# The first 512 tokens of x, loaded two tokens to a partition

## The chip, the cores and the metric

The kernel runs on one core of a Trainium2 chip. The metric is the device time of one launch in microseconds (us). The core has five engines with an instruction stream each: TensorE (PE; its weight loads are shown apart as PEld), VectorE (DVE), ScalarE (ACT), GpSimd (POOL) and SyncE (SP). SP and ACT also issue the DMA transfers, which 16 DMA engines carry out.

## The reference

The computation mixes a memory-augmented attention layer and a gated feed-forward layer, token by token, with a gate. There are 2048 tokens of width 512 in bf16; the attention has 32 heads of width 16 and 4 segments of 512 tokens, the feed-forward a width of 1792.

```python
x = A_x                                                # 2048 x 512
g = sigmoid((x * gate_w).sum(-1, keepdims=True))
a = attention(x)                                       # below
b = (gelu(x @ w_gate) * (x @ w_up)) @ w_down
out = g * a + (1 - g) * b
# attention: q, k, v = x @ wq, x @ wk, x @ wv, in 32 heads; for each segment s of 512 tokens:
p = softmax(q_s @ k_s.T / 4 + causal mask);  a_dot = p @ v_s
a_mem = phi(q_s) @ M / (phi(q_s) @ z + 1e-6)           # phi(t) = t + 1 if t > 0 else exp(t)
o_s = sigmoid(beta) * a_mem + (1 - sigmoid(beta)) * a_dot
M += phi(k_s).T @ v_s;  z += phi(k_s).sum(0)
a = concat(o_s) @ wo
```

## The kernel before

The work goes segment by segment (512 tokens each): projections to q, k and v, scores and softmax, memory, feed-forward, output. Every step is a task with the buffers that it reads and writes. The order in which tasks are given to the engines is written out by hand in a long string, `ORDER` (line 1004), with the PSUM bank or the engine behind a colon: `xev0_00:a` is the task `xev0_00` on ScalarE, `xev0_03:d` is one on VectorE. Each engine runs its own tasks in that order. From the buffers' keys the class `Emitter` works out the semaphore waits of each instruction; it waits for every key that it reads.

All weight matrices lie in SBUF with the contraction index on partitions. Each segment's x is needed transposed, as `xT[...]`: width on partitions (4 blocks `kb` of 128), tokens in the columns. Segments 1 to 3 get it by transposing DMA loads (`ld_xt`, line 355). The first segment is loaded as it is, and TensorE transposes it, which is the part that the change touches:

- Lines 361 and 362: four loads, `x0_0` to `x0_3`, of 128 tokens each (128 KB) into the staging buffer `pt[5]`, a tile of 128 partitions by 4 by 512. Load q puts token 128q + p on partition p, in the q-th 512 columns: 1024 bytes to a partition. The loads 0 and 2 are issued on SP, 1 and 3 on ACT. Each writes the key `("xs", q)`.
- Lines 363 to 367: `wk` in three loads (`wk0` on SP, `wk1` on ACT, 128 KB each; `wk2`, 256 KB, on SP), then `wq` in two loads on SP. By `ORDER`, SP issues x0_0, wk0, x0_2, wk2, wq0, wq1, then wv, which waits for x0_2, and ACT issues x0_1, wk1, x0_3.
- Lines 391 to 393: `wake`, nine matmuls of constants on TensorE ahead of everything else.
- `turn_x0` (line 895): for each half h of the segment (256 tokens) and each block kb, a task `xtr0_{h}{kb}` of two transposes on TensorE (q = 2h and 2h + 1) into two neighbouring 128-column pieces of PSUM, and a task `xev0_{h}{kb}` that copies the 256 columns to `xT[0][:, kb, 256h : 256h + 256]` (line 907 on ScalarE, line 908 on VectorE).
- `project` (line 499): for the first segment, the tasks `K0_k0` to `K0_k3` (line 504) multiply block i of `wk` with the first half's 256 columns, one task for each block i, into four banks; `K0_0b` to `K0_3b` (line 510) do the same for the second half. K0_k0 needs wk0, K0_k1 wk1, K0_k2 and K0_k3 need wk2.

On TensorE the order is wake, the eight transposes of the first half, K0_k0, K0_k1, the eight of the second half, K0_k2, K0_k3, then the K0_*b tasks, the projections to q (line 482) and so on. On ScalarE it is xev0_00, xev0_01, xev0_02, xev0_13, xev0_11; on VectorE xev0_03, xev0_10, xev0_12.

Of the kernel before, what the change touches and what calls it, by code (L numbers as in the profile page):

```python
# [252 lines left out]
def _build(es, nc, A_x, A_wq, A_wk, A_wv, A_wo, A_beta, B_w_gate, B_w_up, B_w_down, gate_w, out):  # L253
    def sb(name, shape, dtype=BF):
        return es.enter_context(nc.sbuf_tensor(name, shape, dtype))
# [4 lines left out]
    xT = [sb(f"xT{i}", [P, 4, 512]) for i in range(R_XT)]  # L260
# [12 lines left out]
    pt = [sb(f"pt{i}", [P, 4, 512]) for i in range(R_PT)]  # L273
# [10 lines left out]
    ident = sb("ident", [P, P])  # L284
# [33 lines left out]
    def program(exact):  # L318
# [3 lines left out]
        def task(name, ways, lat):  # L322
            return S.add(Task(name, ways, lat))

        def one(name, eng, est, instrs, lat=None):
            if lat is None:
                lat = {PE: L_PE, ACT: L_ACT, DVE: L_DVE, POOL: L_POOL, SP: 0.0}[eng]
            return S.add(Task(name, [(eng, est, instrs)], lat))
# [7 lines left out]
        def load(name, eng, fn, writes, issue=0.52, lat=2.5, size=0.0, wait=()):  # L336
            t = one("ld_" + name, eng, issue, [I(fn, [*wait, *late], [*writes, ("ld", name)], sem("s_" + name))],
                    lat=lat)
            t.size = size
# [7 lines left out]
        stage = (R_PT - 1,)  # L347
# [4 lines left out]
        def ld_w(name, eng, dst, src, writes, size, wait=()):  # L352
            load(name, eng, lambda e: e.dma_start(dst, src), writes, size=size, wait=[("ld", w) for w in wait])  # L353
# [5 lines left out]
                    x_of(s % R_XT, kb), issue=1.31, size=0.28, wait=[("ld", behind)])  # L359

        for q, eng in enumerate((SP, ACT, SP, ACT)):
            ld_w(f"x0_{q}", eng, pt[stage[0]][:, q, :], A_x[0, 128 * q:128 * q + 128, :], [("xs", q)], 0.125)
        for h, (eng, c) in enumerate(((SP, slice(0, 1)), (ACT, slice(1, 2)), (SP, slice(2, 4)))):
            ld_w(f"wk{h}", eng, wk[:, c, :], wsrc(A_wk)[:, c, :], [("wk", i) for i in range(c.start, c.stop)],
                 0.125 * (c.stop - c.start))
# [529 lines left out]
        def turn_x0():  # L895
            xs = pt[stage[0]]
            xbf = XALL.bitcast(BF)
            for h in range(2):
                for kb in range(4):
                    key, at = ("Xq", kb), 1024 * kb  # L900
                    one(f"xtr0_{h}{kb}", PE, 2 * T_TR, [I(lambda e, q=q, kb=kb, at=at + 128 * (q % 2): e.transpose(
                        xbf[:, at:at + 128], xs[:, q, kb * 128:(kb + 1) * 128], ident[:, :]),
                        [("xs", q), ("pt", stage[0]), ("ident",)], [key]) for q in (2 * h, 2 * h + 1)])
                    dst, src = xT[0][:, kb, 256 * h:256 * h + 256], xbf[:, at:at + 256]
                    wr = [("xT", 0, kb, 2 * h), ("xT", 0, kb, 2 * h + 1)]
                    task(f"xev0_{h}{kb}", [
                        (ACT, 0.33, [I(lambda e, dst=dst, src=src: e.activation(dst, src, ACTF.Copy), [key, ("X", s0)], wr)]),
                        (DVE, 0.2, [I(lambda e, dst=dst, src=src: e.tensor_copy(dst, src), [key, ("X", s0)], wr)])], L_DVE)

        turn_x0()  # L910
        head_gates()
        for s in range(NSEG):
# [15 lines left out]
        return S, outs  # L928

    S, outs = program(False)  # L930
    order = S.schedule()
    parts = []
    for turn_ in (order, program(True)[0].in_turn()):
        began = {e: len(em.streams[e]) for e in ENGINES}
        for t, eng, instrs in turn_:
            for spec in instrs:
                em.plan(eng, spec)
        parts.append({e: slice(began[e], len(em.streams[e])) for e in ENGINES})
# [175 lines left out]
```

## Time and profile before

| | us |
|---|---|
| Median of 3 runs (265.3, 265.38, 657.67) | 265.38 |
| The profiled execution | 265.2 |
| Its span, first to last instruction | 263.5 |
| TensorE busy in the span | 254.5 |
| ScalarE busy in the span | 209.6 |
| VectorE busy in the span | 204.3 |
| GpSimd busy in the span | 95.7 |

The profile shows one execution. Times in it count from the start of the span, 1.7 us less than the execution as a whole. A row of the timeline gives start, duration, engine, line (L901 is line 901 of the kernel), operation, output and input tiles, and, in brackets, how long the engine sat idle before it and what ended that. `SPq` and `ACTq` are the DMA issues of SP and ACT. The chain of waits follows the work that ended last back from the last instruction: at each step to what released it, or to the instruction before it on its engine. A row by line gives the shortest, median and longest duration in ns. The windows view gives, for a stretch of time, the busy time of each engine in the order PE, PEld, DVE, ACT, POOL, the granted clock of TensorE, the mean busy share of the DMA engines and the GB/s that they moved. Tile names leave out buffer numbers: `pt<-in_A_x_dram` is a load of x into the staging buffer.

### The profile page before, as it was taken

What the parts mean: (1) busy time and instruction counts of PE and PEld (TensorE: products, weight loads), DVE (VectorE), ACT (ScalarE), POOL (GpSimd) and SP (SyncE); (2) the same over time, 40 slices, a digit from 0 to 9 for tenths busy, and PEclk for the clock granted to TensorE, in tenths of its full rate; (3) what the DMA queues carried; (4) which work ended last, traced back from release to release, by engine and by line L of the source; (5) the groups of instructions that cost most, each with busy time, mean ns of one, the idle gap of its engine ahead of it and who ended that gap; (6) DMA issues with size and microseconds to landing.
All of it is one profiled execution on the core that took longest, in us unless ns stands there. A gap on an engine that the chain in (4) does not pass through costs nothing.

```text
span 263.5 us, 6622 instructions
## 1 busy us (share of the span) xinstructions
PE 254.5 (97%) x2792; PEld 113.3 (43%) x2830; DVE 204.3 (78%) x391; ACT 209.6 (80%) x174; POOL 95.7 (36%) x159
## 2 busy tenths in 40 slices
PE   8999999999999999999999999999999999999995
PEld 4633434444344453434434344444344443434343
DVE  1756672989969578998799987797889596877775
ACT  4488989989898998999989697749879988387512
POOL 6007405062643206017262737422734036153600
PEclk9999999999999999999999999999999999999999
DMA  7987179910047301001003000000001000000102
GB/s 225 251 171 215 38 109 203 252 51 2 0 73 106 51 15 40 2 24 40 2 11 74 0 2 2 26 27 2 0 29 49 2 0 2 22 20 2 40 2 85
DMA packets 24702, 14.95 MB, mean 57 GB/s; under 512 B 14558, under 2 KB 24158, under 8 KB 24670
## 3 DMA queue, kind: packets, MB, share of 16 engines
q1 hardware_dynamic: 24094, 14.04, 24.1%
q8 instruction: 23, 0.38, 0.6%
q10 hardware_dynamic: 576, 0.46, 0.5%
q14 instruction: 9, 0.07, 0.1%
HBM read 8.14 MB, written 2.10 MB: 39 GB/s over the span
## 4 chain that ended last, share of the span: by engine, by line
PE 90%; DVE 5%; issue 2%; DMA 2%; SPq 0%
PE psD L482 49%; PE psD L830 19%; PE psX L638 8%; PE psD L691 7%; PE psD L847 5%; DVE gb L817 2%; DMA wk<-in_A_wk_dram 2%; PE psD L510 1%; DVE ost L851 1%; DVE tT L552 1%; SPq L353 0%; DVE phk L495 0%; PE psD L579 0%; PE psD L451 0%; PE psX L597 0%
## 5 line engine op out<-in xcount | busy, mean ns | idle before, releaser
L654 ACT ACTIVATE pt<-psX 128x2048 bf16<-128x2048 f32 x72 | 135.2, 1877 | 30.2 <-PE psX L638 28.5
L660 POOL TENSOR_TENSOR pt<-pt,ctri 128x256 bf16<-128x256 bf16 x128 | 90.5, 714 | 152.8 <-ACT pt L654 148.2
L482 PE MATMUL psD<-xT,wu 128*128 128x512 bf16 x213 | 54.6, 380 | 1.5 <-issue 1.1
L482 PE MATMUL psD<-xT,wg 128*128 128x512 bf16 x216 | 53.5, 380 | 1.0 <-issue 0.6
L830 PE MATMUL psD<-wd,gb 128*128 128x512 bf16 x217 | 53.0, 379 | 0.9 <-issue 0.8
L817 DVE TENSOR_TENSOR gb<-psD,gb 128x512 bf16<-128x512 f32 x56 | 37.3, 683 | 9.4 <-PE psD L482 9.3
L552 DVE STREAM_TRANSPOSE tT<-psD 128x512 f32<-128x512 f32 x35 | 24.2, 707 | 14.7 <-PE psD L691 12.0
L830 PEld LDWEIGHTS psD<-wd,gb 128*128 128x128 bf16 x224 | 20.7, 98 | 26.0 <-issue 2.8
L482 PEld LDWEIGHTS psD<-xT,wg 128*128 128x128 bf16 x224 | 20.5, 98 | 26.3 <-issue 2.6
L482 PEld LDWEIGHTS psD<-xT,wu 128*128 128x128 bf16 x224 | 20.1, 98 | 25.8 <-issue 3.7
L638 PE MATMUL psX<-qT,kD 32*128 32x192 bf16 (+7 forms) x512 | 28.5, 287 | 0.0
L638 PEld LDWEIGHTS psX<-qT,kD 32*128 32x128 bf16 x512 | 8.2, 92 | 25.7 <-ACT pt L654 21.1
L691 PE MATMUL psD<-pt,vnat 64*17 64x128 bf16 (+7 forms) x512 | 18.8, 283 | 0.0
L703 DVE SCALAR_TENSOR_TENSOR ob<-tT,gq,rcall 128x256 bf16<-128x256 f32 x32 | 17.9, 559 | 1.1
L691 PE MATMUL psD<-pt,vsh 64*17 64x128 bf16 (+7 forms) x512 | 18.3, 283 | 0.0
L851 DVE SCALAR_TENSOR_TENSOR ost<-psD,gtok,wds 128x512 bf16<-128x512 f32 (+1 forms) x18 | 12.2, 685 | 6.4 <-PE psD L847 6.2
L482 PE MATMUL psD<-wv,xT 128*128 128x512 bf16 x63 | 16.7, 380 | 0.2 <-issue 0.2
L482 PE MATMUL psD<-xT,wq 128*128 128x512 bf16 x58 | 15.6, 379 | 0.8 <-issue 0.6
L847 PE MATMUL psD<-wo,oT 128*128 128x512 bf16 (+1 forms) x69 | 15.5, 355 | 0.5 <-issue 0.3
L691 PEld LDWEIGHTS psD<-pt,vnat 64*17 64x17 bf16 x512 | 11.6, 86 | 8.6 <-POOL pt L660 3.8
L808 ACT ACTIVATE gb<-psD 128x512 bf16<-128x512 f32 x28 | 14.8, 605 | 0.5 <-PE psD L482 0.2
L475 DVE CAST gb<-psD 128x512 bf16<-128x512 f32 x17 | 11.7, 688 | 4.3 <-PE psD L482 4.3
(99 smaller groups left out, 257.9 us busy)
## 6 DMA issues: line engine op xcount, KB each, us to landing
out_dram<-ost SPq DMA_DIRECT2D x15, 128.0 KB, 1.7
wg<-in_B_w_gate_dram SPq DMA_DIRECT2D x2, 896.0 KB, 6.7
wu<-in_B_w_up_dram SPq DMA_DIRECT2D x2, 896.0 KB, 5.6
wd<-in_B_w_down_dram SPq DMA_DIRECT2D x2, 896.0 KB, 7.6
vsh<-vnat SPq DMA_DIRECT2D x16, 68.0 KB, 2.1
wq<-in_A_wq_dram SPq DMA_DIRECT2D x2, 256.0 KB, 4.7
wv<-in_A_wv_dram SPq DMA_DIRECT2D x1, 512.0 KB, 4.7
pt<-in_A_x_dram SPq DMA_DIRECT2D x2, 128.0 KB, 3.1
```

The lines of the kernel that those rows point to most:

```text
L482: one(f"{name}{'abcd'[h // 2]}", PE, 2 * T_MM, [I(lambda e, i=i: e.matmul(BK[sl.i][:, :], lhs(i), rhs(i), start=(i == 0), stop=(i == n - 1 ...
L552: one(f"tp{name}", DVE, 0.605, [I(lambda e, ts=ts, bank=bank: e.transpose(tT[ts.i][:, :], bank()), [key], [("tT", ts)])])
L638: ins.append(I(lambda e, c=c, kb=kb, ncol=ncol, c0=c0, g=g: e.matmul(XALL[:, g * 512 + c0:g * 512 + c0 + ncol], kD[b][quad(g), c, kb, :], ...
L654: one(f"exp{s}_{name}", ACT, 2048 * 0.000833 + 0.05, [I(lambda e: e.activation(pt[slot][:, :, :], xin, ACTF.Exp, scale=ATT_SCALE), [("X", ...
L660: ins.append(I(lambda e, mv=mv: e.tensor_tensor(mv, mv, cm, ALU.mult), [("pt", slot), ("causal",)], [("pt", slot)]))
L691: ins.append(I(lambda e, kb=kb, slot=slot, c0=c0, n=n, g=g, c=c, r0=r0, sl=banks[j], va=va: e.matmul(BK[sl.i][32 * c:32 * c + 17, 64 * kb: ...
L703: I(lambda e, ts=ts, t=t, j=j, dst=dst, r=r: e.scalar_tensor_tensor(out=dst, in0=t_rows(ts, 16), scalar=gq[:, 2 * t + j:2 * t + j + 1], in ...
L808: one(f"gd{s}_{ft}", ACT, 0.485, [I(lambda e, gi=gi, f=f, sl=sl: e.activation(gb[gi][:, f, :], BK[sl.i][:, :], ACTF.Gelu_apprx_tanh), [bk( ...
L817: one(f"h{s}_{ft}", DVE, 0.605, [I(lambda e, sl=sl, gi=gi, f=f: e.tensor_tensor(gb[gi][:, f, :], BK[sl.i][:, :], gb[gi][:, f, :], ALU.mult ...
L830: mm.append(I(lambda e, fb=fb, gi=gi, f=f, q=q, sl=sl: e.matmul(BK[sl.i][:, :], gb[gi][:, f, q], wd[:, fb, :], start=(fb == 0), stop=(fb = ...
L847: one(f"wo{s}_{qt}_{ci}", PE, 4 * T_MM / len(parts), [I(lambda e, kb=kb, q=q, so=so, c=c: e.matmul(BK[so.i][:, c], oT[:, kb, q], wo[:, kb, ...
L851: lambda e, so=so, gt=gt, wi=wi, oi=oi, c=c: e.scalar_tensor_tensor(out=ost[oi][:, c], in0=BK[so.i][:, c], scalar=gtok[:, gt:gt + 1], in1= ...
```

## The change

The load q now takes the tokens 256h to 256h + 255 (h = q // 2) two to a partition: partition p gets the tokens 256h + 2p and 256h + 2p + 1, which are neighbours in memory, so 2048 bytes in one piece. Of the 128 partitions load q covers one half: q even 0 to 63 on SP, q odd 64 to 127 on ACT. Each load still has 128 KB, and the four are issued in the same places.

A transpose of piece q therefore reads partitions that two loads have filled, and names both keys. Its 128 columns are now every second token of the half, so the copy to `xT[0]` writes the 128 columns of the first transpose to the even columns of the 256 and those of the second to the odd ones; it reads PSUM in order, as before. The string `ORDER`, all later tasks and the other loads are unchanged.

```diff
         for q, eng in enumerate((SP, ACT, SP, ACT)):
-            ld_w(f"x0_{q}", eng, pt[stage[0]][:, q, :], A_x[0, 128 * q:128 * q + 128, :], [("xs", q)], 0.125)
+            h, r = q // 2, slice(64 * (q % 2), 64 * (q % 2) + 64)
+            ld_w(f"x0_{q}", eng, pt[stage[0]][r, 2 * h:2 * h + 2, :],
+                 A_x[0, 256 * h:256 * h + 256, :].rearrange("(p j) d -> p j d", j=2)[r], [("xs", q)], 0.125)
...
-                        [("xs", q), ("pt", stage[0]), ("ident",)], [key]) for q in (2 * h, 2 * h + 1)])
-                    dst, src = xT[0][:, kb, 256 * h:256 * h + 256], xbf[:, at:at + 256]
+                        [("xs", 2 * h), ("xs", 2 * h + 1), ("pt", stage[0]), ("ident",)], [key])
+                        for q in (2 * h, 2 * h + 1)])
+                    dst = xT[0][:, kb, 256 * h:256 * h + 256].rearrange("p (t j) -> p j t", j=2)
+                    src = xbf[:, at:at + 256].rearrange("p (j t) -> p j t", j=2)
```

## The prediction

> **What bounds the kernel now.** I read the page first, then the chain of waits in its first 14 us, then the timeline, the windows and the rows by line for the stage that the change touches. The page:
>
> ```profile
> span 263.5 us, 6622 instructions
> ...
> PE 254.5 (97%) x2792; PEld 113.3 (43%) x2830; DVE 204.3 (78%) x391; ACT 209.6 (80%) x174; POOL 95.7 (36%) x159
> ...
> PE 90%; DVE 5%; issue 2%; DMA 2%; SPq 0%
> ```
>
> TensorE is busy for 254.5 of 263.5 us and carries 90% of the chain that ended last. DMA is on that chain for 2% only, and the chain in order of time shows where:
>
> ```profile
> 1.71 0.43 SPq L353
> 2.14 0.04 issue
> 2.18 4.37 DMA wk<-in_A_wk_dram
> 6.55 0.05 issue
> 6.60 1.05 PE psD L504 x8
> 7.64 1.75 PE psD L510 x16
> ```
>
> So nothing before 6.60 us is bound by TensorE: the last load of wk (wk2, 256 KB) is. From 6.60 us on the chain runs from matmul group to matmul group. A microsecond won before 6.60 us moves all that follows; after that point the change touches nothing. The timeline shows what else could hold TensorE there:
>
> ```profile
> 3.54 0.84 PEld L901 LDWEIGHTS psX<-ident,pt 128*128 128x128 bf16 x8 [0.24 <-DMA pt<-in_A_x_dram]
> ...
> 4.68 0.66 ACT L907 ACTIVATE xT<-psX 128x256 bf16<-128x256 bf16 x2 [0.26 <-PE psX L901]
> ...
> 5.12 0.33 PEld L504 LDWEIGHTS psD<-xT,wk 128*128 128x128 bf16 x4 [0.26 <-ACT xT L907]
> ...
> 5.76 0.39 PEld L901 LDWEIGHTS psX<-ident,pt 128*128 128x128 bf16 x7 [0.20 <-DMA pt<-in_A_x_dram]
> ...
> 6.15 0.52 DVE L908 COPY xT<-psX 128x256 bf16<-128x256 bf16 x2 [1.39 <-PE psX L901]
> ...
> 6.60 1.05 PE L504 MATMUL psD<-xT,wk 128*128 128x256 bf16 x8 [0.26 <-DMA wk<-in_A_wk_dram]
> ...
> 7.37 0.32 PEld L510 LDWEIGHTS psD<-xT,wk 128*128 128x128 bf16 x3
> ```
>
> The loads of x are awaited twice, at 3.54 and 5.76 us, but TensorE then waits once more for wk2 (0.26 us idle). The wait for wk2 ends last; the x path has 0.26 us to spare behind it. Rates, from the windows view (DMA share and GB/s stand last):
>
> ```profile
> 2.00:3.00 1.00, 1.00 (x4) 0.38 (x3) 0.00 (x0) 0.79 (x1) 0.71 (x6) 1.00 0.88 267
> ...
> 4.00:5.00 1.00, 1.00 (x11) 0.71 (x8) 0.29 (x1) 0.70 (x3) 0.82 (x6) 1.00 1.07 329
> ...
> 10.00:12.00 2.00, 2.00 (x11) 0.88 (x9) 2.00 (x8) 1.47 (x4) 0.00 (x0) 1.00 1.00 353
> ```
>
> The engines are full from 3 us on. At 4 to 5 us all packets are rows of 1024 bytes (329 GB/s); at 10 to 12 us most are the 1792-byte rows of wg (353 GB/s). Larger packets move faster.
>
> **The change, part by part.**
>
> *Packets.* The packet records behind the DMA view have these medians: 1024 bytes 46 ns, 1792 bytes 74 ns, 3584 bytes 140 ns. The last two give 66 ns for 1792 more bytes, so a packet costs about 8 ns beside its bytes, and 2048 bytes take 83.5 ns. Each of the 16 engines carries 32 KB of x: before, 32 packets by 46 = 1.47 us; after, 16 by 83.5 = 1.34 us. Gain 0.14 us, and wk2 stands behind all of x in the two queues (SP: x0_0, wk0, x0_2, wk2; ACT: x0_1, wk1, x0_3), so it lands 0.14 us earlier.
>
> Bounds of this. On the good side: from the first packet (1.87 us) to 6.60 us are 4.73 us, and the 64 packets of an engine explain 2.94 us of them; the landing records show wk2 complete on its first engine at 5.35 us and on its last at 6.60, so much is stall. If all of that time went by packets, wk2 would come over a microsecond earlier, and TensorE's own order would bound: the wake matmuls end at 3.56 us, so the transposes could start 0.12 us before their second one of now (3.72 us), K0_k1 would move from 5.12 to 5.00, end its issue at 5.45, eight transposes by 55 ns follow, and K0_k2 starts at 5.9: 0.7 us gained at most. On the bad side: each load now writes 64 partitions only. The nearest rows are the vsh copies, also to 64 partitions: packets of 544 bytes with median 36 ns, where the line between 256 bytes (18 ns) and 1024 bytes (46 ns) gives 28.5, a factor 1.26. By it x takes 1.34 by 1.26 = 1.69 us, 0.2 us more than now. And were the writes of a half held to half rate throughout, x would take 2.68 us: 1.2 us more. I take the gain of 0.14 us: x comes from HBM, like the rows it was worked out from, and both halves are in flight together, which the vsh copies rarely are; 0.7 gained and 1.2 lost stay as ends.
>
> [...]
>
> *Both halves awaited.* A transpose of the first half now needs x0_0 and x0_1. The first transpose started at 3.54 on x0_0 alone, the second at 3.72 on x0_1; the other six follow at 0.107. Now the first waits to 3.72 less 0.07 (half of 0.14) = 3.65, and the eighth comes 0.03 to 0.1 us later than now. Behind it are queued xev0_01 (ScalarE, 4.68), K0_k1 (5.12) and the transposes of the second half (5.46). These wait for x0_3, at 5.76 less 0.14 = 5.62, so a start at 5.56 is hidden. No price; without cover it would cost 0.1 us. In the second half both loads were needed before any eviction already. wv waits for x0_2 on SP's queue (5.14) and beta, wg0 and the transposing loads of x1 behind it; wv is awaited by V0_3a at 12.68, and its successor was issued on its landing at 9.82, so some tenths either way are covered by 2.9 us.
>
> *Issue.* Four issues stay four, in the same places of SP's and ScalarE's queues (0.39 to 0.45 us each); nothing moves past another. Issues in the first 14 us take 0.37 to 0.47 us whatever their rows, so 0.05 us either way each; wk2's issue ends at 2.6 us while its data flow after 4.5 us. No price.
>
> *Evictions.* The count stays at five on ScalarE and three on VectorE; the writes step by 4 bytes instead of 2.
>
> ```profile
> L907 ACT ACTIVATE xT<-psX x5: 378/384/385, 4.0 to 6.3; 128x256 bf16<-128x256 bf16 x5
> ...
> L908 DVE COPY xT<-psX x3: 292/292/293, 4.5 to 6.4; 128x256 bf16<-128x256 bf16 x3
> ```
>
> No row has such a step. ScalarE wrote vnat in short runs in 0.59 us against 0.60 for dense qT, so I take 0 for it, and half as much again (0.19 us) as the bad end. For VectorE, 512 f32 take 0.69 us and 256 bf16 0.29, less than half; at the f32 rate of about 1.04 ns an element 256 need about 0.42, so up to 0.13 each. No row gives a gain. Cover: the second half's evictions end at 6.70 and are wanted at 7.37 (K0_2b), 0.67 us for two in a row on each engine; the first half's gate K0_k1, after which 0.3 us of waiting for x0_3 and 0.26 for wk2 follow. No price; it would decide only if each took 0.3 us more.
>
> **Sum.** 0.14 us less of 265.2 (the profiled execution: span 263.5, 1.7 around it): 265.06. The median of the runs shown, 265.38, is 0.18 above that execution, so the forecast is 265.38 - 0.14 = 265.24, written 265.2.
>
> **Rivals.**
> 1. *Hidden anyway*: wk2's last engine lags by stalls, not by packets (5.35 to 6.60 us between engines speaks for it; the higher rate at 10 to 12 us against). Then wk2 lands at 6.60 as now: 265.4.
> 2. *The half-partition writes collide* (the other side). Engines that had 128 partitions to spread over now meet in 64; the vsh rows speak for it, the two concurrent halves against. x0_3 and wk2 come 0.2 to 1.2 us later, and it decides as soon as the factor on a 2048-byte packet passes 1.10 (92 / 83.5). 265.6 to 266.6; middle 265.8.
> 3. *TensorE's slow start lasts longer.* Transposes start every 107 ns at 3.8 to 4.4 us and every 55 ns at 5.8 us, so the array runs at half pace until about 4.4 us, though the granted clock reads 1.00. A longer gap before the first transpose could put that off. If K0_k0, K0_k1 and the second transposes ran at half pace, 0.87 + 0.44 = 1.3 us, less the 0.26 and 0.14 that wait anyway: 266.3. The gap is only 0.1 us longer, hence a small chance. [...]
> 4. *Startup gains*: fewer rows to set up shortens the stalls as well, 0.4 to 0.7 us: 264.7 to 265.0.
>
> **How the numbers follow.** Forecast (a gain of 0.05 to 0.4) 0.42; hidden 0.22; collision 0.20; slow start 0.05; startup 0.07; anything else, with a wait later in the fixed order that shifts by more, 0.04. The range 264.6 to 266.2 takes in the forecast, the hidden case, the startup gain and most of the collision; left out are its worst end, most of the slow start and half of the unnamed: about 0.12. A difference of 2% is 5.3 us, about what a measurement of this kernel can tell from no change; every case named stays below 1.3 us, so within 2% gets 0.96, faster 0.01, slower 0.03 from the unnamed.
>
> **What would show it.** Right: K0_k2 (line 504, the second group of eight) starts near 6.46 us with a wait for wk before it, x awaited near 3.65 us, 256 fewer packets under 2 KB, DVE's line 908 up to 0.42 us with no waiter moved, and span 263.3 to 263.4. Wrong: x landing later than 3.72 and 5.76 us (rival 2), TensorE waiting at 504 or 510 for line 907 or 908 (evictions dear), transposes of the second half at 107 ns (rival 3), or a first 14 us that gains and an end that does not.

## The result, and the profile after

The change made the kernel slower: 266.61 us median (266.32 to 267.99, 8 executions) beside 265.40 (lowest 265.14), a ratio of 1.0047 with a 95% interval of 1.0033 to 1.0060. That is 1.2 us of loss, well within 2%, but on the other side of the forecast of 265.2 and outside its range. A second comparison of the same kernel gave 1.0062 (1.0035 to 1.0088), with executions from 265.55 to 269.16. One of the eight executions of the kernel before took 657.67 us and is left out of the ratio.

The profiled execution is the slowest of its eight (267.99), so it shows the causes larger than they usually are; of the executions above 268 us no profile was taken. Its page:

```profile
span 266.2 us, 6622 instructions
...
PE 256.2 (96%) x2792; PEld 114.4 (43%) x2830; DVE 204.6 (77%) x391; ACT 210.0 (79%) x174; POOL 95.6 (36%) x159
...
PE 92%; DVE 5%; issue 2%
```

TensorE is busy 1.7 us longer with the same 2792 matmuls, and DMA has gone from the chain that ended last. The chain in order of time (start, duration, what) shows what came instead:

```profile
0.84 2.72 PE psX L393 x9
3.56 0.77 issue
4.33 1.01 PE psX L903 x8
5.34 1.80 PE psD L506 x8
7.14 0.63 issue
7.77 1.01 PE psX L903 x8
8.78 1.63 PE psD L506 x8
10.41 1.75 PE psD L512 x16
12.16 0.05 issue
12.21 1.89 PE psD L484 x8
```

The lines have moved down by two to four: 903 is the transposes, 506 the first half's K0, 512 the second half's, 484 the projections. Before, the first projection (line 482) started at 9.44 us; now at 12.21, 2.77 later, and the span has grown by 2.7. All that follows is shifted as it is; the loss lies in the first 12 us. Two things are to be seen there. TensorE stands idle after the wake matmuls (0.77 us) and again ahead of the second transposes (0.63). And the same work takes it longer: the 16 matmuls of K0 on the first half, in two groups of eight, take 1.80 and 1.63 us, where the second group took 1.05 before. In the timeline:

```profile
0.80 0.60 SPq L353 DMA_DIRECT2D pt<-in_A_x_dram  x1
...
0.81 0.58 ACTq L353 DMA_DIRECT2D pt<-in_A_x_dram  x1
...
1.43 0.86 ACTq L353 DMA_DIRECT2D wk<-in_A_wk_dram  x1
...
4.30 0.78 PEld L903 LDWEIGHTS psX<-ident,pt 128*128 128x128 bf16 x8 [1.01 <-DMA pt<-in_A_x_dram]
...
7.77 1.01 PE L903 MATMUL psX<-ident,pt 128*128 128x128 bf16 x8 [0.63 <-issue]
```

The issues of x took 0.39 and 0.41 us before and take 0.60 and 0.58 now; wk1, behind x on ScalarE's queue, took 0.45 and takes 0.86. x0_3 is issued at 2.33 instead of 1.72. The first packets of x start at 2.19 us on SP's queue and 2.70 on ScalarE's, by the packet records; before, at 1.82 and 2.03. x0_1 has landed at 4.24 us (before: 3.67) and x0_3 at 7.68 (before: 5.72), though fifteen of its sixteen engines were done by 6.43.

Not all of such a difference comes from the change. In the five profiles with loads of 128 partitions by 1024 bytes and unchanged issues (before, and e1, e6, e11 and e12 below), x0_1 landed at 3.67 to 3.95 us, but x0_3 anywhere from 5.72 to 6.94. So one profile's landing of the second half says little; the medians over executions decide.

### The profile page after: what moved, and what is told of

It reads as the page before. It is cut to its first block, busy times and chain, and to the rows that moved or that the text cites. A ratio compares the mean times of both kernels' runs of the same rounds, so it can differ in the third digit from the quotient of the medians.

```text
span 266.2 us, 6622 instructions
## 1 busy us (share of the span) xinstructions
PE 256.2 (96%) x2792; PEld 114.4 (43%) x2830; DVE 204.6 (77%) x391; ACT 210.0 (79%) x174; POOL 95.6 (36%) x159
## 4 chain that ended last, share of the span: by engine, by line
PE 92%; DVE 5%; issue 2%
PE psD L484 48%; PE psD L832 18%; PE psX L640 8%; PE psD L693 7%; PE psD L849 5%; DVE gb L819 2%; PE psD L506 1%; PE psX L393 1%; PE psX L903 1%; PE psD L512 1%; DVE ost L853 1%; DVE tT L554 0%; DVE phk L497 0%; PE psD L581 0%; PE psD L453 0%
```

## The experiments

Three theories. **A**: the idle gap ahead of the first transpose keeps TensorE at half pace for longer. **B**: x and wk land later, because of the partition halves or of the larger packets. **C**: the strided evictions are dear. Each kernel was compared with the kernel before on the same chip in 5 rounds.

### The gap alone, and the gap filled (A against B)

e1 is the kernel before with two wake matmuls fewer; e2 is the change with two more.

```diff
-        for i, cols in enumerate(([512] * 5 + [128] * 3, [128] * 1)):
+        for i, cols in enumerate(([512] * 3 + [128] * 3, [128] * 1)):    # e1
+        for i, cols in enumerate(([512] * 7 + [128] * 3, [128] * 1)):    # e2, e9 to e11, e13 to e15
```

> The kernel before, loads untouched, with two of the five 512-column wake matmuls left out, so that TensorE sits idle for about 0.85 us more ahead of the first transpose, as it does in the changed kernel (0.77 us). Theory A (the idle gap keeps TensorE at half pace for longer): the second half's transposes start every 107 ns and the time is 0.8 to 2 us above the kernel before, about 266.6. Theory B (the loss is the later landing of x alone): TensorE reaches its pace as before or a little later and the time stays within 0.3 us of 265.4. Theory C (dear evictions): no difference either.

> The changed kernel with two more 512-column wake matmuls (0.85 us), so that TensorE is busy until about 4.4 us, when x0_1 landed in the profile (4.30). Theory A: the second transposes start every 55 ns, 0.9 to 1.3 us come back, about 265.5 to 265.8. Theory B: x still lands late, the time stays at 266.4 to 266.8 or gets worse by the longer wake. Theory C: stays at 266.6.

e1: 266.21, ratio 1.0020 (1.0003 to 1.0038), 265.40 to 267.06: a gap alone, with x loaded as before, costs about 0.5 us, less than theory A's number. Its profile shows the mechanism and a reason for the size:

```profile
3.57 1.13 PE L901 MATMUL psX<-ident,pt 128*128 128x128 bf16 x8 [0.86 <-DMA pt<-in_A_x_dram]
4.54 1.89 PE L504 MATMUL psD<-xT,wk 128*128 128x256 bf16 x8
6.80 0.88 PE L901 MATMUL psX<-ident,pt 128*128 128x128 bf16 x8 [0.38 <-DMA pt<-in_A_x_dram]
```

After the gap K0's first group takes 1.89 us, half pace, but the second half of x landed only at 6.75 and 6.94 us in this execution, and TensorE would have waited for it at full pace too.

e2: 266.20, ratio 1.0017 (1.0008 to 1.0025), 265.74 to 266.35: the longer wake takes back 0.30 to 0.45% of the change's 0.47 to 0.62%, some 0.8 to 1.2 us, and the wide spread with it. 0.17% is left, 0.45 us. Both theories hold a part. TensorE's rows of e2:

```profile
4.21 1.06 PE L903 MATMUL psX<-ident,pt 128*128 128x128 bf16 x8
5.18 1.25 PE L506 MATMUL psD<-xT,wk 128*128 128x256 bf16 x8
6.91 0.61 PE L903 MATMUL psX<-ident,pt 128*128 128x128 bf16 x8 [0.48 <-DMA pt<-in_A_x_dram]
7.71 1.05 PE L506 MATMUL psD<-xT,wk 128*128 128x256 bf16 x8 [0.20 <-DMA wk<-in_A_wk_dram]
```

The second transposes take 0.61 instead of 1.01 us, K0's second group 1.05: full pace. What is left are the waits for x and wk, an idle 0.48 and 0.20.

### The halves, the packets and the evictions, one at a time (B and C)

e3 keeps the old token order and dense evictions and takes only the halves: 64 partitions a load, two pieces of 1024 bytes each. e4 takes only the packets (and the evictions that they need): one load of 128 partitions for each half, SP the first, ScalarE the second. e6 takes only the evictions. All three edit the loads of the change:

```diff
-                 A_x[0, 256 * h:256 * h + 256, :].rearrange("(p j) d -> p j d", j=2)[r], [("xs", q)], 0.125)
+                 A_x[0, 256 * h:256 * h + 256, :].rearrange("(j p) d -> p j d", j=2)[r], ...      # e3
+            ld_w(..., pt[stage[0]][:, 2 * h:2 * h + 2, :],                                        # e4, two loads
+                 A_x[0, 256 * h:256 * h + 256, :].rearrange("(p j) d -> p j d", j=2), ...
+            ld_w(..., pt[stage[0]][:, q, :],                                                      # e6
+                 A_x[0, 256 * h:256 * h + 256, :].rearrange("(p j) d -> p j d", j=2)[:, q % 2, :], ...
```

> Only the partition halves of the change: each load covers 64 partitions of a half, as two pieces of 1024 bytes, tokens in the old order, evictions to neighbouring columns as before. Theory B in its form 'halves of the partitions': issues of 0.5 to 0.6 us, x0_1 landing after 4 us, 266.2 to 266.8. Theory B in its form '2048-byte packets': 265.4. Theory C: 265.4. Theory A: follows the landing, over 0.8 us of loss if x0_1 lands 0.5 us later, none if it does not.

> Only the packets of the change: two tokens a partition, 2048 bytes a packet, strided evictions, but each half is one load of all 128 partitions (256 KB, the first on SP, the second on ACT behind wk1), so two issues fewer. Theory B (halves of the partitions): first half landed by 3.7 us, TensorE warm as before, 265.0 to 265.4. If the 2048-byte packets or the evictions (theory C) are the loss: 266 or more. By the prediction's packet price, 0.14 us under the kernel before.

> Only the evictions of the change: loads of 128 partitions with 1024 bytes as before, but load q = 2h + j brings the tokens 256h + 2p + j, so that the evictions step by two columns. Theory C (dear evictions): 0.5 us or more above before. Theories A and B: line 907 near 0.45 us and line 908 near 0.45 us instead of 0.38 and 0.29, time within 0.2 us of before, 265.4 to 265.9.

e3: 267.31, ratio 1.0055 (1.0036 to 1.0074), as slow as the change, with no large packet and no strided eviction. So within the change the halves carry the loss, neither the packets nor the evictions. Their issues, in e3's timeline:

```profile
0.80 0.75 SPq L353 DMA_DIRECT2D pt<-in_A_x_dram  x1
...
0.81 0.73 ACTq L353 DMA_DIRECT2D pt<-in_A_x_dram  x1
```

With as many pieces as the old loads (128 of 1024 bytes) they take 0.75 us instead of 0.39. e4's loads of 128 partitions take 0.39 again, with 2048 bytes a packet.

e6: 265.77, ratio 1.0002 (0.9992 to 1.0012): theory C is out. The evictions did get longer, to 0.46 us on ScalarE and 0.45 on VectorE, in the changed kernel as in e6 (0.45 and 0.44). Nobody waited for VectorE's; TensorE's weight loads waited 0.4 us in all for ScalarE's, in the changed kernel as in e6, after 0.3 before, and e6's time shows no cost of that. Rows by line of the change:

```profile
L911 ACT ACTIVATE xT<-psX x5: 454/459/462, 4.7 to 8.6; 128x256 bf16<-128x256 bf16 x5
...
L912 DVE COPY xT<-psX x3: 444/449/451, 5.2 to 8.8; 128x256 bf16<-128x256 bf16 x3
```

e4: 265.98, ratio 1.0016 (0.9996 to 1.0036), and its executions fall into two groups: six at 265.14 to 265.37 and six at 266.58 to 267.29, with nothing between. Its profile is of the upper group (267.13):

```profile
4.40 1.04 PE L903 MATMUL psX<-ident,pt 128*128 128x128 bf16 x8 [0.84 <-DMA pt<-in_A_x_dram]
5.34 1.89 PE L506 MATMUL psD<-xT,wk 128*128 128x256 bf16 x8
7.02 1.06 PE L903 MATMUL psX<-ident,pt 128*128 128x128 bf16 x8
7.88 1.70 PE L506 MATMUL psD<-xT,wk 128*128 128x256 bf16 x8
```

Half pace until K0's second group, after an idle gap of 0.84 us.

### The same change again, and its partitions spread

> The changed kernel once more, unaltered, to see what of its first profile stays. Theory A+B (64-partition loads take 0.2 us longer to issue and land later, TensorE idles, and keeps half pace): issues near 0.6 us again, x0_1 landed near 4.3 us, 266.2 to 266.9 beside 265.4 to 265.7. If the late last engine of x0_3 (7.7 us, the others by 6.5) was chance, it lands by 6.8 this time.

266.87, ratio 1.0062; the issues were 0.60 and 0.58 us again, x0_1 landed at 3.92 and x0_3 at 6.94, so 7.68 was chance. This execution (266.08) shows the other case of theory A: a gap of 0.46 us, and TensorE at full pace from its first transpose on:

```profile
4.01 0.61 PE L903 MATMUL psX<-ident,pt 128*128 128x128 bf16 x8 [0.46 <-issue]
4.83 1.05 PE L506 MATMUL psD<-xT,wk 128*128 128x256 bf16 x8 [0.21 <-ACT xT L911]
7.03 0.61 PE L903 MATMUL psX<-ident,pt 128*128 128x128 bf16 x8 [1.15 <-issue]
7.47 1.04 PE L506 MATMUL psD<-xT,wk 128*128 128x256 bf16 x8
```

So one and the same kernel doubles its pace before 4.0 us in one execution and only near 10 us in another. The gap was shorter in the first, 0.46 us beside 0.77.

> The change with the 64 partitions of a load spread over the whole tile: even partitions on SP, odd ones on ACT, 2048 bytes a packet. [...] If they lose by the longer issue of a 64-partition transfer, issues stay near 0.6 us and the time at 266.4 to 266.8.

```diff
-            h, r = q // 2, slice(64 * (q % 2), 64 * (q % 2) + 64)
+            h, r = q // 2, slice(q % 2, P, 2)
```

267.47, ratio 1.0058 (1.0033 to 1.0083), issues of 0.56 and 0.62 us: spreading the 64 partitions gives nothing back. In these kernels half the partitions make the issue long, wherever they lie.

### The two groups (A)

> Two loads of 128 partitions, 2048 bytes a packet, strided evictions, and both are the first of their queue (SP the first half, ACT the second, ahead of wk1). Theory A+B: both halves land by 3.9 us, TensorE's idle gap shrinks to 0.3 us, its pace doubles near 4.5 us, 265.0 to 265.4, the only form that could beat the kernel before. If the first half lands at 4.3 us again: 265.7 to 266.2.

> The loads of the full-partition kernel with 2048-byte packets (first half on SP, second on ACT behind wk1), which ran at 265.1 to 265.4 in six executions and at 266.6 to 267.3 in six, with two more wake matmuls, so that TensorE is busy until 4.41 us, when its first half had landed (4.36). Theory A (the two groups are the two moments at which the pace doubles): the upper group disappears, all executions at 265.1 to 265.5, 0.3 to 0.5 us under the kernel before. If the groups have another cause: still two groups 1.5 us or more apart.

> The same loads with x first on both queues, which ran at 267.1 to 267.6, with two more wake matmuls. Theory A: 265.2 to 265.8 in all executions, 1.5 us or more of gain. If the late landing itself (4.5 us for both halves) is the loss: 267.

> The kernel before with two more wake matmuls, so that the first transpose starts at 4.41 us instead of 3.54, as late as in the changed kernel, but with TensorE busy until then. Theory A: at full pace the eight transposes, K0_k0, K0_k1 and the second eight are done by 6.4 us, before wk2 lands at 6.6, so the 0.87 us cost nothing: 265.3 to 265.8. If a late first transpose is dear in itself: 266.2 or more.

e8 is e4 with the second half ahead of wk1 on ScalarE's queue. e9 and e10 are e4 and e8 with the longer wake, e11 is the kernel before with it.

| | median us | range | ratio, interval |
|---|---|---|---|
| e8, x first | 267.39 | 267.11 to 267.56 | 1.0064, 1.0051 to 1.0077 |
| e9, e4 with long wake | 265.21 | 264.98 to 266.04 | 0.9992, 0.9981 to 1.0002 |
| e10, e8 with long wake | 265.61 | 265.28 to 265.96 | 1.0001, 0.9993 to 1.0010 |
| e11, before with long wake | 265.64 | 265.51 to 265.98 | 1.0005, 0.9997 to 1.0014 |

e8 missed its forecast: the halves landed at 4.32 and 4.53 us, not by 3.9, and all five executions took 267.1 us or more. It loses as much as the change with loads of 128 partitions and issues of 0.39 and 0.41 us. What e8, e3, e4's upper group and the change's slowest execution share is a first half that is complete only at 4.24 to 4.42 us, whatever delayed it. Filling e8's gap took 0.63% off, 1.7 us, with the loads unchanged and the first transpose no earlier (e10). TensorE's rows of e8, then those of e10:

```profile
4.37 1.04 PE L903 MATMUL psX<-ident,pt 128*128 128x128 bf16 x8 [0.81 <-DMA pt<-in_A_x_dram]
5.32 1.89 PE L506 MATMUL psD<-xT,wk 128*128 128x256 bf16 x8
7.00 1.06 PE L903 MATMUL psX<-ident,pt 128*128 128x128 bf16 x8
7.85 1.91 PE L506 MATMUL psD<-xT,wk 128*128 128x256 bf16 x8
```

```profile
4.43 1.04 PE L903 MATMUL psX<-ident,pt 128*128 128x128 bf16 x8
5.38 1.56 PE L506 MATMUL psD<-xT,wk 128*128 128x256 bf16 x8
6.77 0.61 PE L903 MATMUL psX<-ident,pt 128*128 128x128 bf16 x8
7.22 1.04 PE L506 MATMUL psD<-xT,wk 128*128 128x256 bf16 x8
```

In e9 e4's upper group is gone. And in e11 the first transpose comes at 4.20 us instead of 3.54 at no cost that can be resolved, since TensorE had work until then:

```profile
4.20 1.06 PE L901 MATMUL psX<-ident,pt 128*128 128x128 bf16 x8
5.10 1.25 PE L504 MATMUL psD<-xT,wk 128*128 128x256 bf16 x8
6.19 0.75 PE L901 MATMUL psX<-ident,pt 128*128 128x128 bf16 x8
7.10 1.05 PE L504 MATMUL psD<-xT,wk 128*128 128x256 bf16 x8 [0.16 <-DMA wk<-in_A_wk_dram]
```

Theory A holds: not the lateness of the first transpose costs most, but the idleness ahead of it. The starts of single matmuls (256 columns every 213 or every 109 ns) give the moment at which the pace doubled in each profile. With the wake of before and a gap of at most 0.5 us behind it, it lies between before 4.0 and 5.2 us (before, e5, e6, e7, e12). With a gap of 0.77 to 0.90 us it lies at 7.3 (e1), 9.2 (e4), 9.8 (e8), 10.0 (e3) and 10.1 us (the change). With the longer wake it lies at 6.5 us or earlier in all seven (e2, e9 to e11, e13 to e15). So in these profiles the late moments go with the long gaps; why, and what a gap between 0.5 and 0.77 us does, no run here shows.

### What the change's rest is, and the remaining steps

> The kernel before, with one edit: each transpose waits for both loads of its half. The prediction priced this at nothing (first transpose at 3.72 instead of 3.54, hidden behind x0_3 and wk2): 265.4 to 265.8, unless the 0.18 us of idling tip TensorE's pace (theory A), then single executions 1 to 2 us above.

265.62, ratio 1.0002 (0.9992 to 1.0012): waiting for both loads of a half costs nothing that could be resolved, as predicted.

> The kernel before with the two more wake matmuls (265.64 in the last comparison, level with before), and one small load (64 bytes to each partition, data that nobody uses) ahead of the first load of x on both queues, so that every load of x and wk is issued about 0.45 us later, as the change does it by its longer issues. If the rest of the loss is issue time: 0.3 to 0.5 us over the kernel before, about 265.9 to 266.1. If it is what half-partition writes do after their issue: within 0.2 us of before.

```diff
+        for q, eng in enumerate((SP, ACT)):
+            ld_w(f"d{q}", eng, ost[q][:, 0:32], A_x[0, 128 * q:128 * q + 128, 0:32], [("ost", q, 0)], 0.01)
         for q, eng in enumerate((SP, ACT, SP, ACT)):
```

266.02, ratio 1.0017 (1.0005 to 1.0030). An issue of 0.39 us ahead of the old loads, with its 8 KB of data and the longer wake, costs about what e2 still lost (1.0017, 1.0008 to 1.0025). Its rows (x is now second in the queue):

```profile
0.80 0.39 SPq L353 DMA_DIRECT2D ost<-in_A_x_dram  x1
1.25 0.42 SPq L353 DMA_DIRECT2D pt<-in_A_x_dram  x1
1.71 0.43 SPq L353 DMA_DIRECT2D wk<-in_A_wk_dram  x1
2.18 0.43 SPq L353 DMA_DIRECT2D pt<-in_A_x_dram  x1
```

> The halves of the partitions with 1024-byte packets and neighbouring-column evictions, with the two more wake matmuls. Issues of 0.6 to 0.75 us, x0 complete at 4.4 us. Theory A: the 1.5 us of loss seen without the longer wake shrink to 0.3 to 0.7 us, 265.9 to 266.3, the rest being the late loads; the 2048-byte packets have no part in it if this rest equals the changed kernel's 0.45 us.

266.16, ratio 1.0020 (1.0007 to 1.0034): the halves without large packets and with the gap filled lose the same rest.

> The full-partition 2048-byte loads with the longer wake once more: 265.0 to 265.4 in most executions, 0.1 to 0.4 us under the kernel before; if the first comparison was chance, level with it.

265.45, ratio 0.9995 (0.9985 to 1.0006). The best form, in its second comparison, is again slightly below the kernel before, and again not by more than the interval: level with it.

## Why the prediction was wrong, point by point

- **The step that failed first: "Issue. ... No price."** It took 0.37 to 0.47 us for any issue, from rows of the first 14 us, all of which fill 128 partitions. The issues of x rose by 0.18 to 0.21 us, wk1's by 0.41, and x0_3's began 0.60 us later. Rows of before gave a warning: the vsh copies, to 64 partitions, took 0.59 to 0.72 us an issue. They were read for their packets and not for their issues. They don't tie it to the partitions, since a load to all 128 partitions took 0.59 us there as well (of wu, at 21.25 us); e3 and e4 do.
- **"Both halves awaited. ... No price"** is right of the wait itself (e12) and wrong of its time: the first transpose was put at 3.65 us and came at 4.30, on x0_1, which had landed at 4.24.
- **Rival 3, the slow start,** was the mechanism of most of the loss. Its price of 1.3 us less what waits anyway (266.3) was near the measured 266.6, in part by luck: it left out K0_k2 and K0_k3, which ran at half pace too (1.63 us for 0.87 in e5), and any later landing. Its chance of 0.05 was not, because it was taken from a gap of 0.1 us where 0.5 to 0.8 came. Of the loss of 0.47 to 0.62%, filling the gap takes back 0.30 to 0.45%, and a rest of 0.17% is about what issuing the old loads 0.4 us later costs (e2 beside e13).
- **Rival 2, collision,** ended on the right side by another mechanism. The change's DMA rate did fall, to 178 GB/s from 4 to 5 us, where the kernel before had 329:

```profile
4.00:5.00 1.00, 0.67 (x7) 0.70 (x8) 0.00 (x0) 0.38 (x2) 0.82 (x6) 1.00 0.92 178
```

  but spreading the partitions (e7) gave nothing back, and a mere delay of the old loads (e13) cost as much with 302 GB/s in that stretch. What the dip is stays open (in e2 it reaches 41 GB/s from 4.5 to 5.0 us); that it costs time beyond the later issue was not seen.
- **"Packets"**: 2048 bytes took 84 ns at the median by the packet records (92 in e5's profile), 83.5 were forecast. That the writes of a half are held to half rate throughout, which the far end of 1.2 us assumes, no run shows: all of these packets went to 64 partitions. The gain of 0.14 us would be 0.05%; e9 and e15 (0.9992 and 0.9995) allow it and do not prove it, and they also have two issues fewer, so that wk2 is issued at 1.71 us instead of 2.18.
- **"Evictions"**: VectorE 0.16 us more each (up to 0.13 forecast), ScalarE 0.08 (0 to 0.19). That they have no price is right, by e6, though in the profiles of e5 and e9 the chain of waits runs through one of ScalarE's (0.47 us).
- **"The last load of wk (wk2, 256 KB) is"** what binds before 6.60 us: true of the execution read. In the profiles of e1, e6 and e12, with loads of the same shape and the same issues, the chain runs through a load of x's second half instead, so 0.14 us for wk2 was not sure to be a gain. Two readings were slightly late: by the records the first packet starts at 1.82 us (put at 1.87), and wk2 lands from 5.30 to 6.55 (put at 5.35 to 6.60). Nothing hangs on them.
- **"A difference of 2% ... about what a measurement of this kernel can tell"**: the intervals here reach 0.1 to 0.3% to either side.
- The limit named in "A microsecond won before 6.60 us moves all that follows" holds for losses: 2.77 us in the profile's first 12 us, 2.7 in its span.

## What to carry to other kernels

Read a DMA's issue time from rows of the same shape (partitions, pieces, bytes a piece), wherever in the trace they are, or measure it, and follow it through every issue behind it on its queue. In the first microseconds ask of every wait not only how long it is, but whether TensorE is left idle before it has reached its pace (here gaps of 0.77 to 0.90 us put that off to 7.3 to 10.1 us); dummy matmuls until the data have landed cost nothing that could be resolved where the data bound anyway (e11, 1.0005). And where a kernel's executions fall into groups, find what separates them before pricing tenths.

## What the runs showed of the hardware

- As the first of its queue, a load to 64 partitions took 0.58 to 0.60 us to issue with 64 pieces of 2048 bytes (the change, e5), 0.73 to 0.75 with 128 of 1024 (e3), and 0.56 to 0.62 with every second partition (e7); a load to 128 partitions took 0.39 to 0.41 with either packet (before, e4, e8). The issues behind the long ones got longer as well (wk1 0.86 us for 0.45). Why, no run shows.
- TensorE's pace (a 128-column transpose every 107 or every 55 ns) is not in the granted clock, which reads 1.00 in the windows from 2 to 8 us at both paces. It doubled between before 4.0 and about 10 us; with the gap filled, the upper of e4's two groups, 1.2 to 2.2 us above the lower, was gone (e9).
- A copy of 256 bf16 from PSUM that writes every second column took 0.46 us on ScalarE instead of 0.38, and 0.45 on VectorE instead of 0.29.
